# Attention with a Fourier MLP on one core: the product with w2 by two levels of the seven-product scheme, its weight combinations streamed from DRAM

## The chip, the core and the metric

The kernel runs on one core of a Trainium2 chip, in one launch, everything in fp32. The metric is the device time of a run in microseconds. The kernel before takes 1631.43 us, the median of three runs (1630.33 to 1632.13). A lower time is better.

## What is computed

```python
# attention: q, k, v are (8, 8, 576, 64), tau is one number
scores = q @ k.T / 8
thresh = max(scores, -1) - tau
scores = where(scores >= thresh, scores, -1e9)
attn = exp(scores - max(scores)); attn /= sum(attn) + 1e-9
x = (attn @ v) as (8, 576, 512)               # heads side by side

# Fourier mixing and the MLP
u = x + real(fft(fft(x, axis=1), axis=2))
un = (u - mean(u)) / sqrt(var(u) + 1e-6)
out = u + relu(un @ w1) @ w2                  # w1 512 x 2048, w2 2048 x 512
```

There are 8 batches of 576 tokens, 4608 tokens in all. The MLP needs most of the arithmetic, and attention comes next.

## The kernel before

**Stages of a batch.** The attention of a batch is 4 pairs of heads times 5 tiles of query rows: 20 steps. Each step makes scores (TensorE, L431), the row maximum (DVE, L455), the exponentials (ACT, L463), the threshold (DVE, L471), transposed weights (TensorE L552, ACT L554) and, twice in a pair, the product with v (TensorE, L581). POOL scales q (L391), copies `rec` for the softmax (L497) and reverses v. When the last pair is done, `mixing(b)` (L653) makes the Fourier transform: folded inputs, the transform along d (TensorE `py` L684, ACT L689), the one along the sequence (`pa` L701 and L705), sum and difference of its two halves (`tmp`, DVE L720), and the sum with x (`u_t`, POOL L723 and L727). `u_t` holds the transposed rows u of two batches in a ring of 1152 columns.

**Groups of tokens.** The MLP takes tokens in groups, in order of their number, across batch borders. The first 384 tokens and the next 128 are done directly (`channels`, L823, with `hidden`, L805). Then come 16 groups of 256 tokens (`channels_in_quarters`, L1051, with `hidden_in_quarters`, L880). These use one level of the seven-product scheme: both factors of a product are cut in 2 x 2 quarters; instead of eight products of quarters, seven products of sums of quarters are made, and the quarters of the result are sums of those. TensorE then makes 7/8 of the columns, and other engines form the sums.

**Product with w1 (hidden).** The result is written in two parts of four banks; each of the seven products has 8 matmuls of 128 columns per part (L918). The sums of token quarters (`t_u`, L892) are made by POOL, those of weight quarters (`s_w`, L901) by DVE or POOL at each use, in place, from w1 which lies in SBUF. They change from group to group in alternating order (`up`), so that each group ends with what the next begins with. The sums of products (L927) are made by DVE, the ReLU (L935) by ACT or DVE, and copies by ACT.

**Product with w2.** The seven products have 8 matmuls of 256 columns each, twice for the halves of tokens: 56 in a group (L1082). Sums of quarters of the hidden values (`s_form`, L1078) are made by POOL and DVE, sums of w2 (`combine`, L1043) by DVE. Each product is scaled with the row's 1/standard deviation and added to u (`Rows.add`, L793, DVE), and finished rows go out (`Rows.store`, L801, SP). `Rows.load` (L770) brings u back in row order: four transposes on TensorE (L774), four copies on ACT, and the statistics on DVE. Its row tiles have two buffers (tag `u`). The PSUM tag `mm` has four banks, for all of mixing and MLP.

**Order of the work.** TensorE executes in program order. In the first two batches every engine does (the hand-written order ends at L1393); after that, a scheduler orders the other engines and only TensorE keeps the program's order. The loop over attention steps calls `fill()` (L1161) three times a step. Each call first advances the current mixing by one stage and then the MLP groups, until the columns spent reach a budget. `start_batch` (L1295) sets the budget: everything that is open, less `keep` (L1305), spread over the 60 calls of the next batch. What is kept back lies between the stages of the next mixing, so that TensorE has work while the Fourier chain waits. A group can start when all its tokens are mixed. After the last batch the loop at the end calls `fill()` until all is done, and three groups of 256 tokens then run with no attention beside them.

Of the kernel before, what the change touches and what calls it, by code (L numbers as in the profile page):

```python
# [47 lines left out]
def kernel(  # L48
# [28 lines left out]
    GT, BT = 384, 256  # L77
    FIRST = 2
    NG = FIRST + (B * S - GT - 128) // BT
    NK = NJ // 2  # L80
# [4 lines left out]
    ps = ctx.enter_context(tc.tile_pool(name="ps", bufs=2, space=bass.MemoryType.PSUM))  # L85

# [172 lines left out]

    pairs_w2 = [const.tile([128, 2 * DM], FP32, name=f"w2_{2 * u}_{2 * u + 1}") for u in range(NK)]  # L260
    w2 = [pairs_w2[j // 2][:, DM * (j % 2) : DM * (j % 2 + 1)] for j in range(NJ)]
# [10 lines left out]
    hs = const.tile([128, NJ * GT], FP32, name="hs")  # L272

    s_w1 = const.tile([128, 2, HID // 2], FP32, name="s_w1")
    t_u = const.tile([128, 3, 2, 128], FP32, name="t_u")
# [51 lines left out]
    def staged(n, src, dst):  # L327
        c0 = 3 * WC * (n % 4)
        stage = hs[:, c0 : c0 + 3 * WC].bitcast(INT32).rearrange("p (c n) -> p c n", c=3)
        return chunk(src, dst, stage[:, 0:2, :], stage[:, 2, :])  # L330
# [9 lines left out]
    def second_chunk(j, room):  # L340
# [4 lines left out]
        if room == "tmp":  # L345
            raw = sb.tile([128, 2 * WC], INT32, tag="tmp", bufs=1, name="stage")[:, :]
        else:
            raw = pairs_w2[int(room)][:, :].bitcast(INT32)
# [304 lines left out]
    def mixing(b):  # L653
# [56 lines left out]

        for t in range(2):
# [36 lines left out]
    def tokens_of(g):  # L748

        if g < FIRST:  # L750
            return ((0, GT), (GT, 128))[g]
        return GT + 128 + BT * (g - FIRST), BT

    def cost(g):

        n = tokens_of(g)[1]
        both = NJ * ND * n + NJ * DM * n // 128
        return 4 * (both if g < FIRST else both * 7 // 8) + ND * n

    class Rows:  # L760


        def __init__(self, g):
            self.first, n = tokens_of(g)
            self.nt = n // 128
            self.us = [None] * self.nt
            self.mv = sb.tile([128, 3, 2], FP32, tag="mv", name="mv")
            self.rstd = sb.tile([128, 3], FP32, tag="rstd", name="rstd")

        def load(self, t):  # L770
# [6 lines left out]
            u = sb.tile([128, DM], FP32, tag="u", bufs=2, name="u")  # L777
# [8 lines left out]
        def factors(self, first, end):  # L786
            rstd = self.rstd[:, first:end]
            nc.scalar.activation(
                out=rstd, in_=self.mv[:, first:end, 1], func=ACT.Sqrt, bias=eps[:, :], scale=1.0
            )  # L790
            nc.vector.reciprocal(rstd, rstd)

        def add(self, t, cols, product):  # L793

            u = self.us[t][:, cols]
            nc.vector.scalar_tensor_tensor(  # L796
# [8 lines left out]
    def hidden(g, count, j, ht):  # L805

        first, n = tokens_of(g)
        c0 = first % RING
        ph = ps.tile([128, 512], FP32, tag="mm", bufs=4, name="ph")

        parts = ((0, n, c0),) if c0 + n <= RING else ((0, RING - c0, c0), (RING - c0, n, 0))
        for a, z, at in parts:
            for c in range(ND):
                nc.tensor.matmul(  # L814
                    ph[:, a:z], w1[c][:, 128 * j : 128 * (j + 1)], u_t[:, c, at : at + z - a],
                    start=(c == 0), stop=(c == ND - 1), skip_group_check=len(parts) > 1,
                )
        if count % 2 == 0:
            nc.scalar.activation(out=ht, in_=ph[:, 0:n], func=ACT.Relu)
        else:  # L820
            nc.vector.tensor_relu(ht, ph[:, 0:n])

    def channels(g):  # L823
        rows = Rows(g)
        n = tokens_of(g)[1]
        h = [hs[:, n * j : n * (j + 1)] for j in range(NJ)]
        for j in range(NJ):
            hidden(g, j, j, h[j])
            yield 4 * ND * n
            if j in (2, 5) and j // 3 < rows.nt:  # L830
                rows.load(j // 3)
                yield ND * 128
            if j == 11:
                rows.factors(0, min(rows.nt, 2))
        if g == FIRST - 1:
            first_sums_w1()
        for t in range(rows.nt):
            po = ps.tile([128, DM], FP32, tag="mm", bufs=4, name="po")
            for j in range(NJ):
                nc.tensor.matmul(  # L840
                    po[:, :], h[j][:, 128 * t : 128 * (t + 1)], w2[j],
                    start=(j == 0), stop=(j == NJ - 1),
                )
                if j % 2 == 1 and j < NJ - 1:
                    yield 2 * 4 * DM
            rows.add(t, slice(0, DM), po[:, :])
            rows.store(t)
            yield 2 * 4 * DM
            if t + 2 < rows.nt:
                rows.load(t + 2)  # L850
                rows.factors(t + 2, t + 3)
                yield ND * 128
# [6 lines left out]

    HH = HID // 2
    a_w1 = [[[w1[2 * k + c][:, HH * i : HH * (i + 1)] for c in range(2)] for k in range(2)]
            for i in range(2)]
    s_u = [s_w1[:, c, :] for c in range(2)]

    def first_sums_w1():  # L870
        for c in range(2):
            tc.keep_in_program_order(nc.vector.tensor_tensor(
                out=s_u[c], in0=a_w1[1][0][c], in1=a_w1[1][1][c], op=ALU.add
            ))
        for c in range(2):
            nc.vector.tensor_tensor(
                out=a_w1[1][0][c], in0=a_w1[0][0][c], in1=a_w1[1][0][c], op=ALU.subtract
            )

    def hidden_in_quarters(g, rows, quarter):  # L880


# [598 lines left out]
```

## Time and profile before

The profiled execution has a span of 1631.3 us from its first to its last instruction; the runs' median is 1631.43.

| stretch (us) | what runs | TensorE busy (us) | DVE | ACT | POOL |
|---|---|---|---|---|---|
| 0 to 214 | first batch of attention, weights arrive | 190.6 | 184.6 | 139.3 | 146.3 |
| 214 to 400 | second batch, first groups | 182.7 | 128.0 | 97.2 | 64.3 |
| 400 to 1442 | batches three to eight with MLP beside them | 1027.7 | 766.2 | 545.1 | 384.3 |
| 1442 to 1476.5 | mixing of the last batch | 32.4 | 18.8 | 5.0 | 14.7 |
| 1476.5 to 1627 | three last groups of 256 | 150.5 | 74.9 | 31.1 | 49.7 |
| 1627 to 1631.3 | last row addition and stores | 0 | 0.9 | 0 | 0 |

A busy share is a mean over stages. Where an engine sets the time, it is busy nearly all the time of the stage. [...] The clock that TensorE was granted is 0.994 of full speed over the span. DMA moved 57.4 MB, 46.0 of them read from DRAM, at a mean of 35 GB/s.

Groups of the page (line, engine, operation | busy us, mean ns of one | idle before, what ended it):

```profile
L463 ACT ACTIVATE e<-sc,neg 128x576 f32<-128x576 f32 x288 | 212.5, 738 | 224.7 <-DVE neg L455 224.5
L1082 PE MATMUL po<-w,hs 128*128 128x256 f32 x1024 | 246.2, 383 | 0.0
L918 PE MATMUL ph<-u_t,w 128*128 128x128 f32 x1536 | 188.1, 277 | 0.0
L1078 POOL TENSOR_TENSOR hs<-hs,s_tile 128x512 f32<-128x512 f32 x32 | 42.0, 1314 | 107.9 <-PE po L1082 85.0
hs<-in_moe_w_ch_dram SPq DMA_DIRECT2D x23, 512.0 KB, 4.8
```

The first row is ACT's largest one; ACT waited 224.5 us for DVE's row maximum ahead of it, which costs nothing while TensorE has other work. The two TensorE rows show no idle time before them. The last row is a DMA: 23 transfers of 512 KB, with a median of 4.8 us from issue to landing.

### The profile page before, as it was taken

How to read it: one execution, taken by the hardware profiler on the slowest of the kernel's cores; microseconds unless marked ns; L12 is line 12 of the kernel's file. 1: busy time of each engine (PE TensorE's matmuls, PEld its weight loads, DVE VectorE, ACT ScalarE, POOL GpSimd, SP SyncE). 2: the span in 40 equal slices, each digit the busy share in tenths (PEclk: the TensorE clock that was granted, in tenths of full speed). 3: DMA queues.
4: the chain of work that ended last, by engine and by line, in shares of the span. 5: the costliest groups of instructions: out<-in, count | busy, mean ns of one | idle time of the engine just before them, and what ended most of it. 6: DMA issues, size and time to landing. Idle time of an engine off the chain costs nothing.

```text
span 1631.3 us, 27898 instructions
## 1 busy us (share of the span) xinstructions
PE 1583.8 (97%) x10346; PEld 1248.7 (77%) x10346; DVE 1173.4 (72%) x2518; ACT 817.8 (50%) x1738; POOL 659.3 (40%) x875
## 2 busy tenths in 40 slices
PE   8998999999999999999999999999999999999998
PEld 4555655577887888878888778877878788889998
DVE  7997886667758686857576868786787869664445
ACT  5765665544455454645445546454636455523111
POOL 6784673042421452244342244224352344124332
PEclk9999999999999999999999999999999999999999
DMA  6423222101110101110011010111111110000000
GB/s 162 123 56 113 74 75 57 40 17 22 20 38 17 34 9 43 23 29 16 21 23 36 17 34 11 41 23 35 17 27 32 22 29 2 14 7 7 14 14 14
DMA packets 203084, 57.41 MB, mean 35 GB/s; under 512 B 193827, under 2 KB 193829, under 8 KB 202950
## 3 DMA queue, kind: packets, MB, share of 16 engines
q1 hardware_dynamic: 200438, 55.34, 14.5%
q8 instruction: 82, 1.34, 0.4%
q10 hardware_dynamic: 2512, 0.30, 0.1%
q14 instruction: 52, 0.43, 0.1%
HBM read 46.02 MB, written 9.44 MB: 34 GB/s over the span
## 4 chain that ended last, share of the span: by engine, by line
PE 77%; DVE 14%; ACT 4%; POOL 2%; issue 2%; DMA 1%; SPq 1%; DVEq 0%; ACTq 0%; POOLq 0%
PE ph L918 24%; PE po L1082 20%; PE pv L581 9%; PE sc L431 7%; PE pw L552 6%; PE po L840 3%; DVE neg L455 2%; DVE e L471 2%; PE ph L814 2%; PE sc L437 1%; ACT e L463 1%; PE pn L774 1%; PE py L684 1%; PE pa L701 1%; DVE hs L1043 1%
## 5 line engine op out<-in xcount | busy, mean ns | idle before, releaser
L463 ACT ACTIVATE e<-sc,neg 128x576 f32<-128x576 f32 x288 | 212.5, 738 | 224.7 <-DVE neg L455 224.5
L455 DVE TENSOR_REDUCE neg<-sc 128x1 f32<-128x576 f32 x288 | 207.3, 748 | 161.6 <-PE sc L431 149.7
L471 DVE SCALAR_TENSOR_TENSOR e<-sc,thr,e 128x576 f32<-128x576 f32 x288 | 229.4, 812 | 42.2 <-ACT thr L467 40.4
L1082 PE MATMUL po<-w,hs 128*128 128x256 f32 x1024 | 246.2, 383 | 0.0
L1082 PEld LDWEIGHTS po<-w,hs 128*128 128x128 f32 x1024 | 186.1, 190 | 33.8 <-issue 12.8
L918 PE MATMUL ph<-u_t,w 128*128 128x128 f32 x1536 | 188.1, 277 | 0.0
L431 PE MATMUL sc<-kT,qT 64*128 64x288 f32 x1024 | 174.4, 433 | 12.6 <-DVE e L471 11.1
L918 PEld LDWEIGHTS ph<-u_t,w 128*128 128x128 f32 x1536 | 180.2, 193 | 5.0 <-issue 3.7
L552 PE MATMUL pw<-ident,e 128*128 128x128 f32 x1152 | 170.7, 275 | 7.8 <-ACT y_o L689 2.3
L554 ACT COPY e_t<-pw 128x512 f32<-128x512 f32 x256 | 148.8, 594 | 48.9 <-PE pw L552 48.2
L927 DVE TENSOR_TENSOR hs<-ph,hs 128x512 f32<-128x512 f32 x160 | 106.9, 685 | 70.7 <-PE ph L918 54.0
L431 PEld LDWEIGHTS sc<-kT,qT 64*128 64x128 f32 x1024 | 96.0, 187 | 78.1 <-issue 37.5
L552 PEld LDWEIGHTS pw<-ident,e 128*128 128x128 f32 x1152 | 134.9, 141 | 27.2 <-ACT y_o L689 4.2
L918 PE MATMUL ph<-t_u,s_w 128*128 128x128 f32 x1024 | 126.7, 277 | 2.1 <-POOL t_u L892 1.8
L918 PEld LDWEIGHTS ph<-t_u,s_w 128*128 128x128 f32 x1024 | 119.9, 192 | 7.4 <-issue 4.6
L1082 PE MATMUL po<-hs,s_tile 128*128 128x256 f32 x512 | 121.5, 381 | 0.0
L796 DVE SCALAR_TENSOR_TENSOR u<-po,rstd,u 128x256 f32<-128x256 f32 (+1 forms) x164 | 75.3, 483 | 63.9 <-PE po L1082 62.8
L492 ACT ACTIVATE e<-e,den 128x576 f32<-128x576 f32 x96 | 74.6, 777 | 76.5 <-DVE den L485 76.0
L1082 PEld LDWEIGHTS po<-hs,s_tile 128*128 128x128 f32 x512 | 94.0, 190 | 13.7 <-issue 2.5
L935 ACT ACTIVATE hs<-hs 128x512 f32<-128x512 f32 x112 | 69.2, 630 | 61.6 <-DVE hs L927 61.6
L614 POOL TENSOR_TENSOR half<-x 128x287 f32<-128x287 f32 x48 | 40.5, 865 | 119.5 <-ACT x L587 61.1
L1078 POOL TENSOR_TENSOR hs<-hs,s_tile 128x512 f32<-128x512 f32 x32 | 42.0, 1314 | 107.9 <-PE po L1082 85.0
(194 smaller groups left out, 2899.5 us busy)
## 6 DMA issues: line engine op xcount, KB each, us to landing
hs<-in_moe_w_ch_dram SPq DMA_DIRECT2D x23, 512.0 KB, 4.8
q_in<-in_q_dram SPq DMA_DIRECT2D x128, 72.0 KB, 2.5
out_dram<-u SPq DMA_DIRECT2D x36, 256.0 KB, 2.2
k_in<-in_k_dram SPq DMA_DIRECT2D x124, 72.0 KB, 2.5
v_in<-in_v_dram SPq DMA_DIRECT2D x64, 128.0 KB, 2.4
w<-in_moe_w_ch_dram SPq DMA_DIRECT2D x6, 512.0 KB, 3.6
stage<-in_moe_w_ch_dram SPq DMA_DIRECT2D x3, 512.0 KB, 3.6
v_in<-in_v_dram SPq DMA_DIRECT2D x64, 16.0 KB, 2.2
```

The source lines that it names most:

```text
L431: nc.tensor.matmul(sc[j][:, c, 0:HALF], qT[hp, 128 * t : 128 * t + 128], kT[hp, k0 + HALF * c : k0 + HALF * (c + 1)], start=True, stop=True,)
L455: nc.vector.tensor_reduce(out=neg[:, j : j + 1], in_=sc[j][:, :, 0:HALF], axis=AXIS_XY, op=ALU.max, negate=True,)
L463: nc.scalar.activation(out=ej, in_=sc[j][:, :, 0:HALF], func=ACT.Exp, bias=neg[:, j : j + 1], scale=1.0)
L471: nc.vector.scalar_tensor_tensor(out=ej, in0=sc[j][:, :, 0:HALF], scalar=thr[:, j : j + 1], in1=ej, op0=ALU.is_ge, op1=ALU.mult, accum_out ...
L492: nc.scalar.activation(out=e[:, S : 2 * S], in_=e[:, S : 2 * S], func=ACT.Copy, scale=den[:, 1:2])
L552: nc.tensor.transpose(pw[:, c, :], e[:, c0 : c0 + 128], ident[:, :])
L554: nc.scalar.copy(e_t[:, 4 * j : 4 * j + 4, qs], pw[:, :, :])
L581: nc.tensor.matmul(pv[64 * j : 64 * j + 64, 0:m], vt[:, 2 * c + j, :], e_t[:, 4 * j + c, 0:m] if c < 4 else ends[:, 0, 0:m], start=(c == 0 ...
L796: nc.vector.scalar_tensor_tensor(out=u, in0=product, scalar=self.rstd[:, t : t + 1], in1=u, op0=ALU.mult, op1=ALU.add,)
L918: nc.tensor.matmul(banks[name][:, 128 * q : 128 * q + 128], left[c][:, 512 * part + 128 * q : 512 * part + 128 * q + 128], right[c], start ...
L927: nc.vector.tensor_tensor(out=to, in0=bank, in1=to if other is None else other, op=ALU.add)
L1082: nc.tensor.matmul(bank[:, 0 : DM // 2], left[p], right[p], start=start and p == 0, stop=p == NK - 1, skip_group_check=True,)
```

## The change

The product with w2 goes by two levels of the seven-product scheme. Groups have 512 tokens, nine in all. The first is done directly. In the other eight:

- The product with w1 keeps one level. Each of its four parts has seven products of 4 matmuls of 256 columns (L1041 of the changed kernel).
- The product with w2 is cut in quarters twice: seven products, each made of seven products of sixteenths, 49 blocks of 4 matmuls of 128 columns (L1168). Sums of the hidden values at the first level are made by `l1_form` (L1090) and at the second by `l2_forms` (L1110). ACT, DVE and POOL take the blocks out of PSUM. `gather` (L1128) and wide additions on POOL (L1209, 128x896, and L1216, 128x1792) put the seven second-level products and then the first-level ones together. `finish` adds the result to u.
- All 7 combinations of w1 and all 49 of w2 are formed once. Those of w1 are made while the first group's product with w2 runs (`w1_forms`, L849: eight POOL additions of 128x1024 at L866). Those of w2 are made while the second group's hidden products run (`w2_forms`, L887: DVE and POOL at L897). They are written to DRAM (`f1`, `f2`) by 35 DMAs on SP. Each of the eight groups reads them back in 20 transfers of up to 1 MB (`ensure`, L944), on SP, into three tiles that held w1; transfer n+2 is issued when the first block of transfer n is used.
- The places of w2 in SBUF hold second-level sums and partial results afterwards, and the fourth w1 tile holds a first-level sum.
- Row tiles have four buffers; the four sums of token quarters of a group share them.
- `settle` runs groups of earlier batches until their rows are loaded, before a mixing writes u_t. What `keep` holds back is 21 blocks (3 of the seven products). Groups seven and eight (counted from zero) both need tokens of the last batch.

The core of the diff:

```diff
-    GT, BT = 384, 256
-    FIRST = 2
-    NG = FIRST + (B * S - GT - 128) // BT
+    BT = 512
+    NG = B * S // BT
...
-            u = sb.tile([128, DM], FP32, tag="u", bufs=2, name="u")
+            u = sb.tile([128, DM], FP32, tag="u", bufs=4, name="u")
...
+    def w1_forms():
...
+        def form(out_, in0, in1, op=ALU.subtract):
             for c in range(2):
-                nc.gpsimd.tensor_tensor(out=out_[c], in0=in0[c], in1=in1[c], op=ALU.subtract)
+                nc.gpsimd.tensor_tensor(
+                    out=quarters[out_][c], in0=quarters[in0][c], in1=quarters[in1][c], op=op
+                )
+
+        keep(1, (0, 0))
+        keep(4, (1, 1))
+        yield
+        keep(2, (0, 1))
+        form((1, 1), (1, 1), (1, 0), ALU.add)
...
+    PER = 4
+    LOADS = [(f1, 28, k) for k in range(0, 28, PER)] + [(f2, 49, k) for k in range(0, 49, PER)]
+    issued = 0
+
+    def ensure(n):
+
+        nonlocal issued
+        while issued <= n and issued < (NG - 1) * len(LOADS):
+            src, count, k = LOADS[issued % len(LOADS)]
+            n_blocks = min(PER, count - k)
+            nc.sync.dma_start(
+                out=w1[issued % 3][:, 0 : 512 * n_blocks].rearrange("p (j n) -> p j n", n=512),
+                in_=src[:, k : k + n_blocks, :],
+            )
+            issued += 1
...
+        u_form(t1, b[0, 1], b[0, 0])
+        u_form(t2, b[1, 1], t1)
+        u_form(minus_t4, b[1, 0], t2)
+        u_form(t3, b[1, 1], b[0, 1])
...
+        for at, m in enumerate(L1):
+            banks = []
+            for jn, j in enumerate(J):
+                if jn in (0, 4):
+                    banks.append(ps.tile([128, 512], FP32, tag="mm", bufs=4, name="po"))
+                to = banks[-1][:, 128 * (jn % 4) : 128 * (jn % 4 + 1)]
+                right_ = block(g, True, 7 * at + jn)
+                for s in range(4):
+                    nc.tensor.matmul(
+                        to, lefts[m][j][:, s], right_[:, 128 * s : 128 * (s + 1)],
+                        start=jn in (0, 4) and s == 0, stop=s == 3, skip_group_check=True,
+                    )
+                if jn == 0:
+                    if m == 4:
+                        l1_form(s1_tile, s1_tile, a11, (V, P, V, P))
+                    if m == 6:
+                        l1_form(a12, a12, s1_tile, (V, P, V, P))
+                    if at < 6:
+                        coming = l2_forms(L1[at + 1])
+                        next(coming)
+                        next(coming)
+                    if m == 2:
+                        l1_form(a21, a11, a21, (P, P, P, P))
+                if jn in (2, 4) and at < 6:
+                    next(coming)
...
+                    if m in (1, 5, 4):
+                        nc.scalar.copy(here({1: v_u, 5: v_22, 4: v_21}[m]), src)
+                    elif m == 2:
+                        V.tensor_tensor(out=here(v_11), in0=here(v_u), in1=src, op=ALU.add)
+                    else:
+                        to = here(v_12 if m == 3 else v_u)
+                        V.tensor_tensor(out=to, in0=to, in1=src, op=ALU.add)
...
+            if m == 2:
+                gather(P, v_11, 1)
+            elif m == 6:
+                P.tensor_tensor(out=v_12, in0=v_u, in1=v_22, op=ALU.add)
+                finish(0, 0, v_11)
+            elif m == 7:
...
+                both = v_22_21.rearrange("p (v n) -> p v n", v=2)
+                P.tensor_tensor(out=both, in0=both, in1=twice, op=ALU.add)
+                gather(V, v_22_21, 2)
+                finish(1, 1, v_22)
+                finish(1, 0, v_21)
+                rows.store(2)
+                rows.store(3)
+            elif m == 3:
+                gather(V, v_12, 1)
+                finish(0, 1, v_12)
+                rows.store(0)
+                rows.store(1)
...
-        keep = 0.4 * cost(0) + cost(1) if b == 0 else 4 * 7 * NK * DM // 2 * BT // 256
+        keep = 4 * BT * NJ * DM // 128 if b == 0 else 3 * 7 * 2048
```

## The prediction

> **What bounds the kernel now.** I read the page first, then the chain of work that ended last, then windows at the batch boundaries, then the timeline of DVE and POOL in the part with no attention work. The page says which engine is full:
>
> ```profile
> PE 1583.8 (97%) x10346; PEld 1248.7 (77%) x10346; DVE 1173.4 (72%) x2518; ACT 817.8 (50%) x1738; POOL 659.3 (40%) x875
> PE   8998999999999999999999999999999999999998
> POOL 6784673042421452244342244224352344124332
> ```
>
> TensorE is busy 97% of the span and has a 9 in nearly every slice, so a column of matmul that is removed is time that is removed, until another engine becomes late. DVE has 28% of the span free, POOL 60%. The end of the chain of waits gives prices that nothing else disturbs (start, length, work):
>
> ```profile
> 1476.50 5.62 PE ph L918 x48
> 1482.12 0.44 PE pn L774 x4
> 1482.56 7.15 PE ph L918 x64
> 1489.71 0.44 PE pn L774 x4
> 1490.14 12.51 PE ph L918 x112
> 1502.65 24.18 PE po L1082 x112
> 1526.83 5.36 PE ph L918 x48
> ```
>
> One group of 256 tokens repeats every 50.0 us (1526.83 to 1576.89 to 1626.98). An fp32 matmul makes two records: 128 columns take 2 x 12.51/112 = 0.2234 us, 256 columns 2 x 24.18/112 = 0.4318 us. Just before, the same chain shows what TensorE waits for after the last Fourier stage, a POOL queue:
>
> ```profile
> 1470.08 0.47 DVE tmp L720
> 1470.62 0.80 POOL u_t L723
> 1471.42 1.40 POOL u_t L727 x2
> 1472.82 1.29 POOL u_t L723 x2
> 1474.11 0.75 POOL u_t L727
> 1474.86 0.43 POOL t_u L892
> ```
>
> The windows at three earlier batch boundaries show TensorE (first figure after the comma) short of 20 us by 1.5 to 1.8 us; the windows after them hold 19.4, 20.0 and 19.8:
>
> ```profile
> 500.00:520.00 20.00, 18.35 (x114) 13.70 (x114) 16.05 (x41) 9.50 (x21) 1.27 (x1) 1.00 0.03 7
> 720.00:740.00 20.00, 18.16 (x130) 14.71 (x130) 11.74 (x23) 6.34 (x16) 10.40 (x18) 0.91 0.07 27
> 920.00:940.00 20.00, 18.47 (x122) 14.46 (x121) 16.07 (x39) 11.35 (x26) 5.47 (x6) 1.00 0.19 31
> ```
>
> The clock column falls to 0.91 in one of them: a stall costs a little more than its length. Last, DVE and POOL beside each other:
>
> ```profile
> 1614.03 3.33 DVE L1043 TENSOR_TENSOR hs<-w,hs 128x512 f32<-128x512 f32 x3 [0.38 <-PE po L1082]
> 1615.01 3.49 POOL L1078 TENSOR_TENSOR s_tile<-s_tile,hs 128x512 f32<-128x512 f32 x2 [0.46 <-PE po L1082]
> ```
>
> Two POOL operations that take 1.27 us each alone (1613.28, same timeline) take 3.49 together, three DVE ones 3.33 instead of about 2.1: they took turns.
>
> **What the Trainium skill says.** "TensorE: Matmul & The Clock Gate", section "Wait — 56ns, not 53.3ns?": N/2.4 GHz plus about 2.5 ns per matmul. The trace agrees if an fp32 matmul is four passes: 4 x 55.8 = 223 ns for 128 columns (measured 223.4), so halving a matmul's width costs only some 10 ns in 223. "GPSIMD Engine Reference", section "3.1 Elementwise — side-by-side cycle accounting": 4497 ns for a two-input add of 2048 elements, 2.2 ns an element; the trace has 1.27 us for 512 and 1.53 for 608, 2.5 ns an element, and I use that. "SBUF — State Buffer", section "Who interferes with whom": a DVE operation with two SBUF inputs and a reading POOL operation exclude each other; the pair above agrees. "DMA: Bandwidth & Descriptors", section "Bandwidth": 1 MB in 6.15 us, 341 GB/s; the trace moves 512 KB in 4.8 us (3.6 when quiet) and reaches 381 GB/s in the microsecond from 59.
>
> **The change part by part**, against the profiled span of 1631.3 us (the median of the runs is 1631.43).
>
> *Columns, -48.9.* 512 tokens cost 2 x 50.02 = 100.04 us. Afterwards: hidden 4 x 7 x 4 = 112 matmuls of 256 columns, 48.3 us; product with w2 7 x 7 x 4 = 196 of 128 columns, 43.8; transposes 4 x 0.44 = 1.8; together 93.9. Eight groups save 8 x 6.15 = 49.2; the first 512 tokens stay direct (+0.3 for other widths).
>
> *Weight sums that disappear, 0.* L901, L1043 and the 128-wide L892 lie beside TensorE now; what takes their room is counted below.
>
> *Streaming, +3 (0 to 15), an estimate.* A group reads 7 + 13 pieces of 1 MB, 160 MB in all, through SP and three of the old w1 tiles, two pieces ahead. A piece feeds TensorE for 16 x 0.2234 = 3.57 us, which is 294 GB/s with no attention between. The 381 GB/s say it is held; two pieces ahead give 7.1 us of cover to a landing of 5 to 6. SP issues in order, so q, k, v and stores queue behind a load that waits for a free tile: the wait is for TensorE's last read of the piece before, at most one piece.
>
> *Last mixing, +8 (4 to 11).* From 1441.6 to 1476.5 the last Fourier stage is filled with 23.3 us of L1082. Kept back afterwards are 21 blocks, 21 x 4 x 0.2234 = 18.8 us, 4.5 less, and by the TensorE order none is left in the pa stage, where the 6.4 us chain quoted above is bare; a gather also stands ahead of its DVE step (2 to 3).
>
> *Group 7 to 8, +7.5 (2 to 12).* Both come free only with the last batch. t_u and the rows u now share four buffers, so t1 of group 8 waits for the stores of group 7's rows: after its last product come POOL's double-width add (L1216 of the changed kernel, 1792 wide at 2.5 ns: 4.4 us), the gather 3.0, finish 1.9 of which part overlaps, the store 2.2. t1 is there at about +7.7 us; TensorE needs it after its first product, at +1.7. That is 6, and 1.5 for the clock.
>
> *w2 stage without attention, +1 (0 to 6).* Sums for the next first-level product just arrive: in 6.3 us per product DVE has 3 to 4 additions, POOL 2 to 6.
>
> *End, +6.6 (5 to 8).* After the last matmul the kernel before needs 4.35 us (1626.95 to 1631.3). Afterwards there are an evacuation, seven dependent gather and finish steps, some 7.5 us at 0.5 to 0.7 each, and 3.4 for the store: 10.9.
>
> *Forms in batch 2, +15 (5 to 25).* In the changed build's instruction order (line numbers of the changed kernel from here) six POOL operations of 128x1024 (L866; 2.45 us each, 15.2 with issue) stand ahead of the copy `rec` of the softmax (0.38 us, L497 before) in POOL's queue. TensorE reaches its use 5.1 us later: about 10 lost, 2 for clock. Behind the eight four-row forms of w2 (L897) stands t2 of group 1: 28.7 us of queue against 27.6 of cover, 1 to 5. If the forms start earlier than I place them, the first part goes.
>
> *Five boundaries, +15 (0 to 30).* At each of batches 3 to 7 the mixing's `tmp`, u_t and t_u steps now share DVE and POOL with the 1792-wide add, the 896-wide ones and the gathers. A boundary has no slack (the 1.5 to 1.8 us above). Half of a 4.4 us operation plus a gather step in front is 3 us: 5 x 3. A boundary may also fall in hidden, where nothing of this stands: 0.
>
> Sum: 1631.3 - 48.9 + 3 + 8 + 7.5 + 1 + 6.6 + 15 + 15 = 1638.5.
>
> **The rivals.**
> *(1) Covered, faster.* POOL is 40% busy; if neither forms nor wide additions stand in front of something TensorE needs, the terms of batch 2, boundaries and streaming vanish: 1631.3 - 48.9 + 8 + 7.5 + 1 + 6.6 = 1605.5. The place is POOL's queue in front of `rec` and u_t; it decides from about 26 us of stalls in these places: above, the gain is gone. For it: the program's fill takes work by a budget, so boundaries can fall anywhere. Against: in-order queue, wide operations.
> *(2) DMA is the bound in w2.* At 250 GB/s a piece takes 4.2 us against 3.57: 13 x 0.62 = 8 in each of the two groups without attention, 1655. For: 160 MB where 57 were moved, besides head-of-line waits. Against: 381 GB/s seen.
> *(3) DVE and POOL exclude each other.* In a w2 stage I count some 51 us of their SBUF work against 47 without attention, 69 against 77 with it, DVE being near 80% in attention. If the softmax is late by 5 us in each of six stages: 1638.5 + 30 = 1668. For: the pair quoted. Against: 14 us of waits in the whole middle of the trace, so steps have slack.
>
> **How the numbers follow.** A measurement tells 0.2% (3.3 us) from no change. Chances: forecast 0.50, rival 1 0.22, rival 2 0.08, rival 3 0.20. The forecast's own range is 1615 to 1660 (its uncertain terms do not all go one way): of its 0.50, 0.08 lie below 1628, 0.09 within 3.3 us of 1631.4, 0.33 above. Faster 0.22 + 0.08 = 0.30, same 0.09, slower 0.61. The range runs from just under rival 1's value, 1603, to just over rival 3's, 1672; about 0.1 is left out on either side.
>
> **What would show it.** Right: in the part after the last attention step a group takes 94 us with ph pairs of 0.4318 and po of 0.2234; a TensorE wait of some 10 us on `rec` in batch 2; windows of 20 us at boundaries with TensorE at 15 to 17; a gap of 6 us between groups 7 and 8; 11 us after the last matmul. Wrong: TensorE waiting on the streamed tiles w1 (rival 2); many short waits on DVE's `e` and `neg` all along (rival 3); none of these (rival 1). If 128-column products with new weights every time were slower than 0.2234, the gain itself falls: 0.01 us is 8 x 196 x 0.01 = 16 us.

## The result and the profile after

The changed kernel takes 1691.78 us (1689.67 to 1693.34), the kernel before in the same comparison 1631.78. The ratio is 1.037 (95% interval 1.035 to 1.038): slower by 60 us, where 1638.5 was forecast and 1672 was the upper end of the range. The profiled execution has a span of 1689.9 us against 1631.3, a difference of 58.6. One run of the experiment e17 below, of 2030.9 us at a granted clock of 0.715, is left out of its median.

The page of the changed kernel, engine totals and TensorE's busy tenths:

```profile
PE 1570.3 (93%) x9770; PEld 1213.6 (72%) x9770; DVE 1178.3 (70%) x2438; ACT 794.6 (47%) x1700; POOL 856.6 (51%) x953
PE   8998888998998899989999999899998999989997
```

TensorE is busy only 13.5 us less, though 49 us of columns are gone, and it is idle for 119.6 us instead of 47.5. The 9s have gaps all along. Its mean granted clock fell from 0.994 to 0.968, which is why the busy time fell so little. DVE's total is as before.

The end of its chain of waits (start, length, work) shows that the gain in columns is there:

```profile
1484.83 49.07 PE ph L1041 x214
1533.90 9.82 PE po L1168 x88
1543.72 0.44 PE pn L763 x4
1544.16 6.25 PE po L1168 x56
...
1564.23 10.73 PE po L1168 x96
1574.98 4.77 DMA w<-f
```

A record of 128 columns takes 6.25/56 = 0.1116 us, as before, and 256 columns keep their 0.216 (the median step from one record to the next). Group 7 occupies TensorE from 1484.83 to 1579.41, 94.6 us. Ten of the 224 records of its hidden product (2.2 us) had run before the wait that ends at 1484.83, and the clock after this wait (mean 0.946 up to 1534) takes 2.7 us. Without wait and slow clock the group needs 94.1 us for 512 tokens, where 93.9 was worked out and the kernel before needs 100.04.

To see where the rest went, cut both traces at the start of each batch's Fourier transform along d (the first `py`), and take from each stretch its MLP matmul records at the undisturbed price (0.1117, 0.2159 and, for 384 and 512 columns, 0.320 and 0.432 us a record). What is left is attention, mixing and waiting:

| stretch | before | after | difference | predicted |
|---|---|---|---|---|
| to the first mixing | 136.9 | 136.8 | 0 | 0 |
| first to third mixing | 179.7 | 208.8 | +29 | +15 (forms) |
| third to eighth (five batches) | 398.2 | 455.7 | +57.5 | +15 (boundaries), +3 (streaming) |
| eighth to the end | 18.5 | 40.7 | +22 | +23 |
| MLP records at undisturbed price | 898.0 | 847.9 | -50 | -48.9 |

The sum is +58.6. The columns and the end came out as forecast. The middle did not. In one of these batches TensorE is idle for 10.1 us (3.2 before), and the granted clock takes another 5.1 (0 before).

The windows at the boundary of the fifth mixing, 20 us each (TensorE's busy time is the first figure after the comma; the clock is third from the end):

```profile
900.00:920.00 20.00, 17.41 (x133) 13.56 (x132) 16.89 (x38) 12.85 (x27) 4.73 (x3) 1.00 0.35 120
920.00:940.00 20.00, 16.06 (x122) 14.23 (x121) 16.19 (x36) 7.67 (x19) 11.10 (x10) 0.93 0.37 102
940.00:960.00 20.00, 20.00 (x115) 15.38 (x114) 15.43 (x31) 8.76 (x19) 15.25 (x26) 0.90 0.45 150
```

The kernel before lost 1.5 to 1.8 us in such a window; here it is 4, and 2.6 in the one ahead. The timelines of POOL, DVE and TensorE there (start, length, line, operation; in brackets the idle time before and what ended it):

```profile
925.69 4.00 POOL L1216 TENSOR_TENSOR w_all<-w_all 128x1792 f32<-128x1792 f32 x1 [2.05 <-DVE w_all L1203]
```

```profile
929.72 4.59 DVE L1128 TENSOR_TENSOR w_all<-w_all 128x256 f32<-128x256 f32 x7 [2.36 <-POOL w_all L1216]
934.23 2.19 DVE L789 SCALAR_TENSOR_TENSOR u<-w_all,rstd,u 128x256 f32<-128x256 f32 x4
936.35 0.51 DVE L484 TENSOR_SCALAR e<-e,den 128x576 f32<-128x576 f32 x1
```

```profile
937.19 0.47 PE L530 MATMUL pe<-ident,e 128*128 128x128 f32 x1 [3.39 <-ACT e L497]
```

DVE stands still for 2.4 us until POOL's wide addition is done, then gathers and finishes for 6.6. The softmax step L484, whose inputs are ready at 926.6, comes after them in DVE's order, and TensorE waits for it. Four more waits repeat in every batch, of 1.0, 2.4, 1.3 and 1.3 us, each on the softmax (`e` or its transposed copy `e_t`) and each beside the product with w2. The longest one seen from DVE, POOL and TensorE:

```profile
874.60 1.65 DVE L1090 TENSOR_TENSOR hs<-hs,w 128x512 f32<-128x512 f32 x1
...
877.52 1.75 DVE L1110 TENSOR_TENSOR w_all<-hs,w_all 128x512 f32<-128x512 f32 x1
```

```profile
875.65 1.73 POOL L1090 TENSOR_TENSOR w<-w,hs 128x512 f32<-128x512 f32 x1
```

```profile
881.13 1.23 PE L427 MATMUL sc<-kT,qT 64*128 64x288 f32 x6 [2.38 <-DVE e L467]
```

Sums of 0.69 us take 1.7 here, beside sums on POOL, and L467 follows them. DVE is never idle from 868 us to this L467, so here it does not wait for POOL: it is slowed.

### The profile page after: what moved, and what is told of

Its sections match the earlier page's. It is cut to its first block, busy times and chain, and to the rows that moved or that the text cites. A ratio compares the mean times of both kernels' runs of the same rounds, so it can differ in the third digit from the quotient of the medians.

```text
span 1689.9 us, 27055 instructions
## 1 busy us (share of the span) xinstructions
PE 1570.3 (93%) x9770; PEld 1213.6 (72%) x9770; DVE 1178.3 (70%) x2438; ACT 794.6 (47%) x1700; POOL 856.6 (51%) x953
## 5 line engine op out<-in xcount | busy, mean ns | idle before, releaser
L467 DVE SCALAR_TENSOR_TENSOR e<-sc,thr,e 128x576 f32<-128x576 f32 x288 | 228.8, 812 | 47.9 <-ACT thr L463 46.6
L1041 PE MATMUL ph<-t_u,w 128*128 128x256 f32 x1024 | 245.5, 386 | 9.6 <-POOL t_u L997 9.3
L1168 PE MATMUL po<-w,w_all 128*128 128x128 f32 x1792 | 242.1, 288 | 5.9 <-ACT ends L540 5.3
L1168 PEld LDWEIGHTS po<-w,w_all 128*128 128x128 f32 x1792 | 226.9, 203 | 15.3 <-issue 7.8
L1041 PEld LDWEIGHTS ph<-t_u,w 128*128 128x128 f32 x1024 | 188.7, 192 | 42.9 <-POOL t_u L997 11.3
L1110 POOL TENSOR_TENSOR w_all<-hs 128x512 f32<-128x512 f32 x72 | 100.3, 1395 | 225.4 <-PE po L1168 122.9
L427 PE MATMUL sc<-kT,qT 64*128 64x288 f32 x1024 | 177.3, 434 | 25.8 <-DVE e L467 24.8
L1041 PE MATMUL ph<-u_t,w 128*128 128x256 f32 x768 | 186.0, 387 | 6.3 <-ACT hs L1052 5.6
L1010 DVE TENSOR_TENSOR hs<-ph,hs 128x512 f32<-128x512 f32 (+1 forms) x128 | 105.0, 821 | 114.3 <-PE ph L1041 114.3
L548 PE MATMUL pw<-ident,e 128*128 128x128 f32 x1152 | 172.8, 277 | 6.2 <-ACT u L769 2.9
L1041 PEld LDWEIGHTS ph<-u_t,w 128*128 128x128 f32 x768 | 143.9, 193 | 34.5 <-issue 8.6
L548 PEld LDWEIGHTS pw<-ident,e 128*128 128x128 f32 x1152 | 138.4, 143 | 23.5 <-issue 5.7
L1168 PE MATMUL po<-w,hs 128*128 128x128 f32 x960 | 128.7, 281 | 0.0
L1168 PEld LDWEIGHTS po<-w,hs 128*128 128x128 f32 x960 | 119.2, 196 | 5.9 <-issue 5.5
L484 DVE TENSOR_SCALAR e<-e,den 128x576 f32<-128x576 f32 x120 | 89.6, 747 | 3.7
```

The costliest lines, as they stand in the source:

```text
L427: nc.tensor.matmul(sc[j][:, c, 0:HALF], qT[hp, 128 * t : 128 * t + 128], kT[hp, k0 + HALF * c : k0 + HALF * (c + 1)], start=True, stop=True,)
L467: nc.vector.scalar_tensor_tensor(out=ej, in0=sc[j][:, :, 0:HALF], scalar=thr[:, j : j + 1], in1=ej, op0=ALU.is_ge, op1=ALU.mult, accum_out ...
L484: nc.vector.tensor_scalar(out=e[:, 0:S], in0=e[:, 0:S], scalar1=den[:, 0:1], scalar2=None, op0=ALU.mult)
L548: nc.tensor.transpose(pw[:, c, :], e[:, c0 : c0 + 128], ident[:, :])
L1010: nc.vector.tensor_tensor(out=to, in0=bank, in1=to if other is None else other, op=ALU.add)
L1041: nc.tensor.matmul(bank[:, 256 * q : 256 * q + 256].rearrange("p (two n) -> p two n", two=2), left[:, 256 * c + 128 * q : 256 * c + 128 * ...
```

## The experiments

My theory after this reading: the loss is DVE's in-order queue, in which sums that wait for POOL stand ahead of softmax steps (queue theory). The rivals: sums of POOL and DVE that run at the same time hold each other up (exclusion theory, rival 3 of the prediction), DVE's load is too high by itself, and the stream. All times are medians, with the ratio to the kernel before beside them. That kernel took 1631.8 to 1633.4 us in these comparisons, so differences of 1 or 2 us between rows say nothing.

| run | us | ratio (95%) |
|---|---|---|
| the change | 1691.8 | 1.035 to 1.038 |
| e1 wide addition on DVE | 1687.2 | 1.032 to 1.035 |
| e2 first-level sums on DVE | 1671.0 | 1.022 to 1.026 |
| e3 forms of w1 on DVE | 1682.9 | 1.029 to 1.033 |
| e4 no streamed loads | 1691.2 | 1.034 to 1.037 |
| e5 gather later | 1692.2 | 1.033 to 1.037 |
| e6 = e2, scratch additions on POOL | 1671.5 | 1.022 to 1.026 |
| e7 clock kept up | 1686.5 | 1.031 to 1.034 |
| e8 = e2 + e3 + e5 | 1664.9 | 1.018 to 1.021 |
| e9 no sums in w2's product | 1592.3 | 0.973 to 0.976 |
| e10 = e8, boundary earlier | 1634.5 | 1.000 to 1.002 |
| e11 = e8, w2 spread out | 1670.3 | 1.021 to 1.025 |
| e12 = e8, own t1 | 1664.0 | 1.018 to 1.021 |
| e13 boundary earlier, alone | 1662.6 | 1.017 to 1.019 |
| e14, e15 = e8 with six, four kept | 1678.8, 1658.5 | 1.027 to 1.031, 1.014 to 1.017 |
| e16 = e10 and two more | 1625.9 | 0.995 to 0.997 |
| e17 POOL's sums only | 1623.0 | 0.991 to 0.996 |
| e18 DVE's sums only | 1600.9 | 0.979 to 0.982 |

### Single steps: e1 to e4

```diff
-                P.tensor_tensor(out=both, in0=both, in1=twice, op=ALU.add)
+                V.tensor_tensor(out=both, in0=both, in1=twice, op=ALU.add)
```

> The 128x1792 addition of product 7 (L1216) is made by DVE instead of POOL. Queue theory (at a batch boundary DVE's in-order queue waits for POOL's 4.0 us addition before its gather, and the softmax step L484 stands behind both): the DVE idle time of 2.4 us ahead of the gather goes and the addition itself falls from 4.0 to about 2.3 us, so TensorE's wait of 3.3 us ahead of L530 falls to 1 us or less at six boundaries, with 3.4 us of slow clock each where it was long: 1660 to 1678. Exclusion theory ([...]their total work is the bound): DVE has 2.3 us more to do where it is full already, and the time stays within 1688 to 1698.

4.5 us less, and between the two expectations. DVE at the same boundary:

```profile
923.08 2.02 DVE L1216 TENSOR_TENSOR w_all<-w_all 128x1792 f32<-128x1792 f32 x1
925.01 0.45 DVE L717 TENSOR_TENSOR tmp<-pa,tmp 128x289 f32<-128x289 f32 x1
925.38 3.64 DVE L1128 TENSOR_TENSOR w_all<-w_all 128x256 f32<-128x256 f32 x7
928.94 1.66 DVE L789 SCALAR_TENSOR_TENSOR u<-w_all,rstd,u 128x256 f32<-128x256 f32 x4
```

The wait for POOL is gone and the gather is shorter (3.64 against 4.59), but the additions are still ahead of L484, which now runs at 932.35, and TensorE waits 3.8 us instead of 3.4 (for the last part on ACT, where L497 stands behind two exponentials until 934.16). It was not the wait for POOL alone that held the softmax up here.

```diff
-                        l1_form(s1_tile, s1_tile, a11, (V, P, V, P))
+                        l1_form(s1_tile, s1_tile, a11, (V, V, V, V))
...
-                        l1_form(a12, a12, s1_tile, (V, P, V, P))
+                        l1_form(a12, a12, s1_tile, (V, V, V, V))
```

> The first-level sums of products 4 and 6 (L1090) are made by DVE alone instead of by DVE and POOL in turn. Exclusion theory (DVE's L1090 takes 1.7 us instead of 0.7[...]): the TensorE wait of 2.4 us on L467 behind them falls to about 1 us in five batches, and its slow clock goes: 1675 to 1685. Theory that DVE's queue is simply too long in the product with w2: two more additions of 0.69 us for each sum, the wait grows by 1 to 2 us: 1693 to 1705.

20.8 us less. That is the direction of the exclusion theory, and more than it expected, although DVE has more to do: its L1090 additions take 64.4 us (30.6 + 33.8) instead of 38.1. What fell is its idle time ahead of the second-level sums of the first-level sum (busy, mean ns | idle before, releaser), in the changed kernel and in e2:

```profile
L1110 DVE TENSOR_TENSOR w_all<-w_all,w 128x512 f32<-128x512 f32 x16 | 15.2, 952 | 49.6 <-POOL w_all L1110 35.6 <-PE pe L530 14.0
```

```profile
L1110 DVE TENSOR_TENSOR w_all<-w_all,w 128x512 f32<-128x512 f32 x16 | 11.9, 742 | 21.5 <-PE pe L530 14.0 <-POOL w_all L1110 7.5
```

28 us of waiting for POOL at the head of DVE's queue are gone. The sums are also stretched less: 32 more of them, 22 us at 0.69 each, make DVE's busy time only 8 us longer (1186.1 against 1178.3). So the run does not decide between the two theories; its trace shows one in each of two places. A wait of 5.3 us that ends at 515 us, behind an idle time of DVE of 4.9 us for POOL, became 1.4. The wait of 2.4 us on L467 became 0.7 in each of four batches; DVE is not idle ahead of this L467 in either kernel, but two of its sums now take 2.4 us together:

```profile
1051.77 2.36 DVE L1090 TENSOR_TENSOR hs<-hs,w 128x512 f32<-128x512 f32 x2
```

A new wait of 1.4 us, ahead of L1168, comes behind it in these batches.

```diff
-                nc.gpsimd.tensor_tensor(
+                nc.vector.tensor_tensor(
                     out=quarters[out_][c], in0=quarters[in0][c], in1=quarters[in1][c], op=op
                 )
```

> The eight additions of 128x1024 that form w1's combinations (L866) are made by DVE instead of POOL. If they held up the copy rec in POOL's queue in the second batch, as the prediction said, TensorE's wait of 5.4 us ahead of L533 and the slow clock after it go: 1680 to 1685. If another wait ends last there, or if DVE's softmax steps are held up instead: 1689 to 1694.

8.9 us less. The wait of 5.4 us ahead of L533, on `rec`, is gone, with the slow clock behind it. This mechanism of the prediction was right.

```diff
-            nc.sync.dma_start(
+            if issued < 20: nc.sync.dma_start(
```

> Leaves out the streamed loads of the groups after the second: each group reads what the 20 transfers of the first streamed group left in the three tiles, so the products use wrong weights. DMA theory (streams delay TensorE, or q, k, v and the stores queue behind them on SP): 1650 to 1680. My theory (transfers land in 4.9 us and TensorE waits for one of them once, 0.5 us): 1688 to 1693, no difference.

No difference: 141 MB of streaming cost nothing that can be measured.

### The boundary's queue and the clock: e5 to e8

e5 turns the gather of product 7 into a generator and advances it from the third block of product 3 on.

```diff
-                gather(V, v_22_21, 2)
-                finish(1, 1, v_22)
-                finish(1, 0, v_21)
-                rows.store(2)
-                rows.store(3)
+                waiting = last_rows()
...
+                if jn > 1:
+                    next(waiting, None)
                 if jn < 6:
                     yield 2048
```

> The gather and finish of product 7 are asked for later, from the third block of product 3 on instead of at the end of product 7; in the order of DVE's instructions the softmax step L484 now stands just ahead of the gather instead of behind it. Nothing else is changed. Queue theory (the boundary's stall is L484 standing behind a gather that itself waits for POOL): TensorE's wait of 3.3 us ahead of L530 falls below 0.5 us at six boundaries and its slow clock, some 3.4 us each, goes too: 1655 to 1672. Theory that DVE has simply too much work at the boundary: the wait moves to the next user of DVE (tmp, the row maximum) at the same length: 1686 to 1694.

No gain. The 3.4 us ahead of L530 and 0.6 on `tmp` became 2.0 ahead of L548 and 2.1 on `tmp` L718. Here the other expectation is right: at the boundary DVE has too much to do at once (busy 9.97 of the 10 us from 930), and the order only says who waits.

```diff
+                    if m in (4, 6):
+                        idle_pool()
```

> As the experiment with the first-level sums on DVE alone, but POOL makes four additions of 512 elements per group to a scratch tile beside them, which nobody waits for. If that experiment gained because DVE no longer shared its ports with POOL (exclusion theory), DVE's additions are stretched to 1.7 us again and the gain is lost: 1684 to 1694. If it gained because DVE's queue no longer waited for sums that POOL made late (queue theory), the gain stays: 1669 to 1676.

No change, but this run tells nothing: the scheduler put the scratch additions elsewhere, none of them beside DVE's sums, whose mean stayed at 985 and 1075 ns. No later run puts this question again: in e17 POOL's sums meet DVE's softmax, but not DVE's sums.

```diff
+        if i >= 60 and i % 20 == 4:
+            twice = bass.AP(
+                tensor=ones.tensor, offset=ones.offset, ap=[list(ones.ap[0]), [0, 2], [1, 128]]
+            )
+            for _ in range(8):
+                nc.tensor.matmul(pe[:, 2:4, :], ones[:, :], twice, start=True, stop=True)
         nc.tensor.transpose(pe[:, 0, :], e[:, 512:640], ident[:, :])
```

> TensorE makes eight more fp32 matmuls of 256 columns (3.45 us by 0.4318 us each), on constants into PSUM columns that nobody reads, ahead of L530 at five of the boundaries, in the place where it stood still for 3.3 us. If the slow clock after the stall costs 3.4 us each time, as the windows after 933 us show (0.70, 0.50 and 0.66 of full speed for 3 us each), it is gained: 1673 to 1678. If the slow clock costs nothing because other engines are waited for in that time anyway: 1690 to 1694.

5.2 us less, a third of what was expected. In the batch from 903 us the clock stayed at 1.00, a gain of 5.1 us by the windows, and the wait of 3.4 us was filled, yet idle time stayed at 10.0 us: waits of 0.7 and 1.8 us came up ahead of L530 and L1168 in the next product with w2. In that batch most of the time gained from the clock turned into new waits.

e8 joins the edits of e2, e3 and e5.

> First-level sums on DVE, w1's combinations formed by DVE, and the later gather, together. If the three stalls are apart from each other, gains add: 1691 - 20.8 - 8.9 and - 20 to - 35 for the gather, 1627 to 1643, about the kernel before. If DVE becomes the bound when it carries all of it: above 1655.

26.9 us less; 20.8 and 8.9 nearly add, e5 adds nothing. The kernel before is not reached: the boundary is left.

### What the sums cost: e9, e17, e18

e9 leaves out the second-level sums except for product 1, L1090, the gathers and the joining additions.

```diff
         def l1_form(out_, in0, in1, engines):
+            return
...
-                eng.tensor_tensor(out=out_, in0=in0, in1=in1, op=op)
+                if m == 1:
+                    eng.tensor_tensor(out=out_, in0=in0, in1=in1, op=op)
...
         def gather(eng, v, n):
+            return
```

> The changed kernel without the additions that serve the two levels in the product with w2: no second-level sums of hidden values except for product 1, no first-level differences (L1090), no gather and no joining additions (L1209, L1216); the output is then not the reference's. TensorE's work, the streams and the evacuations stay. If DVE's and POOL's additions in that stage hold TensorE up: a batch takes about 173 us instead of 184.5, and the whole 1605 to 1630. If the cost lies elsewhere (streams, 128-column products, forms): above 1660.

99.5 us less than the change and 41 less than the kernel before. A batch takes 169.4 us. So TensorE's side of the scheme is worth what was worked out, and the loss of the five middle batches is in the sums: counted as in the table above, those batches take 17.6 us less than in the kernel before. Of its other rows, 18 us between the first and third mixing and 8 at the end remain.

```diff
+                if eng is nc.gpsimd:
+                    eng.tensor_tensor(out=sink[:, :], in0=in0[:, c], in1=in1[:, c], op=ALU.subtract)
```

> As the run without the sums of the product with w2 (1592.3), but POOL makes its share of them, with inputs of the same kind and number, into a scratch tile that nobody reads; DVE's share stays left out, and the output is not the reference's. If DVE and POOL's exclusion of each other holds the softmax up (exclusion theory): 1610 to 1640. If POOL's additions hurt only through those who wait for them (queue theory): 1590 to 1600.

> The counterpart: DVE makes its share of the sums into a scratch tile that nobody reads, POOL's share is left out, and the output is not the reference's. If DVE's load by itself makes the softmax late: 1625 to 1660. If it is the waits of DVE for POOL and back that do: 1592 to 1610, and the rest up to 1691.8 is the chain between the two.

e18 has the same edit with `nc.vector`. DVE's share alone costs 8.5 us. POOL's share alone costs 31 (its gather was replaced by four 512-wide additions, 5.1 us instead of 3.5). That is in the range which was expected for the exclusion theory, but the trace shows another cause. Beside 303 us more of POOL work DVE's busy time grew by 26 us (L484 from 688 to 754 ns, L789 from 510 to 664), and TensorE's waits on the softmax did not grow (9.0 us on L467, 8.9 without). One wait of 6 us in each of four batches is new; what TensorE and then, in one of these batches, SP waited for (us, times, longest):

```profile
PE po L1189 <- DMA w<-f: 25.1, 4, 6.4
```

```profile
SPq L149 <- POOL v_rev L525: 16.2, 1, 16.2
```

A load of v waits on SP for POOL's `v_rev`, which stands behind the additions on POOL, and a streamed tile stands behind that load on SP. The changed kernel's own trace has only one wait of 0.5 us on a streamed tile, so this cost is hardly part of its loss.

The shares alone give at most 8.5 + 31 = 39 of the 99.5 us; the other 60 or more need the sums of both engines. DVE's load by itself and the stream (e4) fall as main causes. But two causes need both engines, and e17 and e18 cannot tell them apart, because each leaves out one side: DVE waits for sums that POOL makes (queue theory), and sums on both engines at once hold each other up (exclusion theory). The changed kernel's trace has both. DVE stands idle for POOL for 71 us ahead of second-level sums (35.6 and 11.4 at L1110) and gathers (24.3 at L1128), and its busy time is 57 us longer than in e18 (1178.3 against 1121.6), where it makes at least as many sums, alone (the first line is of the changed kernel, the second of e18):

```profile
L1128 DVE TENSOR_TENSOR w_all<-w_all 128x256 f32<-128x256 f32 x72 | 42.3, 640 | 24.5 <-POOL w_all L1216 24.3
```

```profile
PE 1534.2 (96%) x9770; PEld 1188.1 (74%) x9770; DVE 1121.6 (70%) x2438; ACT 796.3 (50%) x1700; POOL 565.2 (35%) x737
```

TensorE's five longer waits of the batch from 905 us divide as follows. The one of 3.4 us at the boundary and the one of 1.0 at 1045 come after idle times of DVE, of 2.4 us for L1216 and of 3.5 us for a sum of POOL that ends at 1039.74:

```profile
1038.48 1.26 POOL L1110 TENSOR_TENSOR w_all<-w 128x512 f32<-128x512 f32 x1
1039.78 0.69 DVE L1110 TENSOR_TENSOR w_all<-w_all,w 128x512 f32<-128x512 f32 x1 [3.50 <-PE pe L530]
```

(The view names PE as what ended the idle time; the sum of POOL that DVE's L1110 reads ends at the same moment.) The one of 2.4 us on L467, shown above at 881 us and repeated at 1065, comes after stretched sums without any idle time of DVE. Of the two of 1.3 us, the one at 912 comes after two L789 of 2.71 us together, beside POOL's L1209, and a table load of 1.3 us on ACT, and the one at 1088 after DVE's work for the next mixing. So that both engines are needed is shown; how much of the loss is waiting and how much is stretching is not.

### The place of the boundary: e10 to e16

```diff
-        keep = 4 * BT * NJ * DM // 128 if b == 0 else 3 * 7 * 2048
+        keep = 4 * BT * NJ * DM // 128 if b == 0 else 5 * 7 * 2048
```

> On top of the three changes together (1664.9): five of the seven first-level products are kept back for the next mixing instead of three, so that the batch boundary falls on products 5 and 4, not on 6, 7 and 3 with their wide additions and gathers. If the place of the boundary makes its stall (4 us and as much slow clock in six places): 1625 to 1645. If DVE's work in the whole product with w2 is what counts: 1660 to 1668, the stall shows up elsewhere.

30.4 us less, level with the kernel before. In its trace the mixing from 862 to 895 us meets product 4 and half of product 6, and the wide additions of 6 and 7 come at 901 and 910, behind it. From 862 to 1037 us, one batch, idle time is 5.3 us and the clock 1.00 throughout; in e8 it was 10.0, with 1.7 for the clock.

> The changed kernel (1691.8) with nothing else than the earlier boundary: five first-level products kept back for the next mixing instead of three. If the place of the boundary is the larger part of the loss by itself: 1655 to 1668. If it gained 30 us only because the other three changes had been made: above 1675.

The same edit on the change alone gives 29.2, so it does not need the others.

> The three changes together, with six products kept back. If the stall belongs to the wide additions of products 6, 7 and 3 alone, six are as good as five, 1630 to 1638. If products 5 and 4 have cost of their own that shows when the boundary is on 2 and 5: 1625 to 1632, or worse above 1640 where the sums of product 5 stand in the queue.

> The three changes together, with four products kept back. The boundary falls on products 4, 6 and the start of 7: between 1634 and 1665 if the cost goes with the place; with the wide addition and gather of 7 just behind the mixing, 1640 to 1650.

Four give 6.4 us, six lose 13.9. Of what was expected for six only "worse above 1640" came. Waits of 1.2 to 2.9 us, mostly on the softmax, come back after the mixing's start; which sums stand ahead of it there, I did not follow up. Five is the best of four values. The cost does go with the place, but not with the wide additions alone.

e11 changes the yields of the two products (4096 to 3200, 2048 to 2560).

> On top of the three changes together (1664.9): a block of the product with w2 counts 2560 in the budget instead of 2048, one of the product with w1 3200 instead of 4096, so that w2 is spread over about 11.7 of the 20 attention steps of a batch instead of 9.3. If too many additions per attention step make the softmax late there: 1640 to 1655. If single chains of waits do, whatever the pace: 1660 to 1668.

5.4 us more. Fewer blocks per attention step did not help: e8's loss was not the rate.

```diff
-            sb.tile([128, 512], FP32, tag="u", bufs=4, name=f"t_u{m}")[:, :].rearrange(
+            sb.tile(
+                [128, 512], FP32, tag="u" if m else "t1", bufs=4 if m else 1, name=f"t_u{m}"
+            )[:, :].rearrange(
```

> On top of the three changes together (1664.9): the first sum of token quarters has a buffer of its own instead of one of the four shared with the rows. If group 8 waits for the stores of group 7's rows, as the prediction said: 4 to 6 us less, 1659 to 1661. If the next sums, which still share, wait as long: 1663 to 1666.

0.9 us, not measurable. In e8 the two waits ahead of group 8, for a streamed tile and for t1, were 1.9 + 1.6 us (0.5 + 3.7 in the changed kernel); here they are 0.5 + 0.8.

e16 has e10 and e12, and for the last batch half of the additions to u_t on DVE.

> Five products kept back, the three changes, an own buffer for the first token sum, and for the last batch half of the additions to u_t made by DVE instead of POOL. The wait of 5.9 us ahead of group 7 and those of 1.8 and 2.2 ahead of group 8 shrink by 2 to 5 us together: 1629 to 1633, level with the kernel before or just below.

1625.9 us, 0.4% faster than the kernel before. The wait ahead of group 7 fell from 5.9 in e10 to 2.6.

## Why the prediction was wrong

*Columns, -48.9: right.* Group 7 works out at 94.1 us, and the records give -50.

*Streaming, +3: right within its range.* e4 gives 0. The tile that TensorE waited for cost 0.5 us.

*Last mixing, groups 7 to 8, w2 stage without attention and end, together +23: right, +22.* In parts: 5.5 us were waited for t1 of group 7, 0.5 + 3.7 between the groups, and 9.6 pass after the last matmul, where 10.9 was worked out.

*Forms in batch 2, +15: the mechanism right, the size half.* `rec` behind L866 is real (5.4 us and its clock, 8.9 in e3; 12 was worked out for it). The stretch cost 29, though. Two more waits of TensorE of over 5 us in it, ending at 405 and 515, were not foreseen. Ahead of the first, up to 398 us, DVE's queue waits for a store of the room that L897 reuses, with the row maximum behind it. Up to 510.7 it waits 4.9 us for POOL's second-level sum, which stands there behind L1090; e2 shortened it.

*Five boundaries, +15: this step failed.* It put 3 us on each boundary and, streaming apart, nothing on the rest of a batch; the five batches cost 57.5, 11.5 each, above its upper end of 30. It named the wrong queue. I put POOL's wide addition ahead of `u_t` on POOL; what was late was the softmax on DVE, behind a gather that waits for that addition. And it left the place open ("A boundary may also fall in hidden"), where the diff says it: `keep` holds back three products, so every boundary meets products 6, 7 and 3, the ones with L1209, L1216 and the gathers. Moving it by two products is worth 29 us by itself (e13). Counted as in the table, e13's five batches cost 21 us over the kernel before, so some 37 of the 57.5 go with the place (the end of the kernel loses 5 of them again). For the other 21, waits beside the product with w2, the forecast had no term. The sign that the prediction gave for the boundaries, TensorE at 15 to 17 us in a window of 20, came true (16.1 and 17.4 above); it does not tell POOL's queue from DVE's.

*Rival 3, 1668, was nearest, and part of its reason is there.* Its softmax waits beside w2 are there: 6 us in each batch and some clock, where it said 5 us, and TensorE's waits on `e` ahead of its scores grew from 11.1 us to 24.8. The longest of them, 2.4 us, comes after DVE sums that POOL's sums stretch, as it said. Others, of 1.0 us beside w2 and of 3.4 at the boundary, come after waits of DVE for POOL, which it did not have. That the waits of the middle "have slack" held for attention steps of the kernel before, not for steps with these sums between.

*Slow clock.* I gave a stall 1.5 to 2 us. Windows of 3 us show more after one of 3.4 (936 to 945 in the changed kernel):

```profile
936.00:939.00 3.00, 1.33 (x5) 0.93 (x5) 3.00 (x8) 1.69 (x4) 0.37 (x1) 0.70 0.66 199
939.00:942.00 3.00, 2.94 (x12) 1.80 (x13) 2.90 (x9) 1.80 (x6) 3.00 (x5) 0.50 0.00 0
942.00:945.00 3.00, 3.00 (x20) 3.00 (x20) 1.62 (x1) 0.29 (x1) 3.00 (x6) 0.66 0.03 8
```

That is 0.9 + 1.5 + 1.0 = 3.4 us at the price of columns. By e7 removing it returns about 1 us a boundary. This size was too small by about half.

What stays open: how the 60 us divide between waits of DVE for POOL and sums that the two engines stretch for each other, and why six kept products are worse than five. A run in which POOL's sums stay beside DVE's, but write to a tile that nobody waits for, would divide them.

## What to carry to other kernels

Before a scheme moves work from TensorE to sums on other engines, follow each sum through the in-order queue that it stands in and ask who is behind it, and what the other engine does at the same time. In this case a DVE that is 70% busy stopped TensorE when the head of its queue waited for POOL, and when its sums ran beside POOL's. Where a budget keeps work for a boundary, read from it which part of the work meets the boundary, and put the part with the fewest cross-engine sums there. An ablation that leaves all the sums out (41 us faster than before) tells early whether the scheme is worth tuning.

## What the runs showed of the hardware

After the TensorE wait of 3.4 us that ends at 937.2 the granted clock was 0.50 for 6.8 us, and after the one of 2.4 that ends at 1065.6 it was 0.50 for 3.4 us:

```profile
937.20:944.00 6.80, 6.25 (x26) 4.71 (x27) 6.32 (x13) 3.54 (x8) 5.37 (x8) 0.50 0.26 77
1066.90:1070.30 3.40, 3.40 (x17) 3.40 (x18) 2.77 (x6) 1.03 (x3) 1.58 (x2) 0.50 0.30 45
```

After the waits of 1.3 us in this batch it stayed at 1.00. Length alone does not decide: of two waits of 1.7 us one, at 288 us, was followed by 3.4 us at 0.50 and one, at 206, was not. POOL's wide additions were cheaper per element than its 512-wide ones: 3.98 us for 1792 (2.2 ns, the rate of the Trainium skill's "GPSIMD Engine Reference", section "3.1 Elementwise — side-by-side cycle accounting"), against 1.27 for 512 (2.5 ns). A streamed megabyte landed in 4.9 us at the median, less than the 6.15 us of the Trainium skill's "DMA: Bandwidth & Descriptors", section "Bandwidth"; that figure is for transfers issued from GpSimd, and these were issued from SP.
